# One attention block and one gated feed-forward block on one core: maxima tiles in pairs of banks until the first gate product, and query groups and the first projection as products over all rows

## The chip, the cores and the metric

The kernel runs on 1 core of one Trainium2 chip. Its engines are called as the profile calls them: PE (TensorE, the matrix products), PEld (TensorE's loads of weights), DVE (VectorE), ACT (ScalarE), POOL (GpSimd) and SP (SyncE, whose queue issues nearly all DMAs here). The time of a run is the device time in microseconds (us) of one execution. Half a per cent of this kernel's time is some 8 us.

## The reference

One layer on 2048 rows of width 512: an attention with 32 heads of 16 columns, which share one key and one value head, then a feed-forward block with 1792 gated columns. Each has a layer norm before it, which is scaled and shifted by vectors that are made from `c`, and a gate vector behind it.

```python
mod = (_silu(c) @ w_mod).reshape(c.shape[0], 6, 1, -1)
sa, ca, ga, sb, cb, gb = (mod[:, i] for i in range(6))      # written out in the source
h = _layernorm(x) * (1 + ca) + sa
q, k, v = (h @ wq, 32 heads of 16), h @ wk, h @ wv          # one k and one v for all heads
o = softmax(q k^T * 16 ** -0.5) v
x = x + ga * (o @ wo)
h = _layernorm(x) * (1 + cb) + sb
x = x + gb * ((sigmoid(h @ w_gate) * (h @ w_up)) @ w_down)
```

The inputs are fp32. The kernel splits operands into two fp16 parts, high and low, and adds three products (high with high, high with low, low with high) where the reference has one.

## The kernel before, in words

**Prologue** (some 105 us): loads, the vectors made from `c`, the first norm, keys, values and the first query groups. Its order stands in a table, PLAN.

**Main loop.** The queries are cut into 8 blocks of 256 rows, the heads into 4 groups of 8; such a pair is a *unit*, 32 in all. A unit has 16 *steps*, one for each 128 keys, so there are 512 steps, and a step has two *half-steps*. A half-step issues on PE, in this order (ORDER):

- `s0`, `s1`: two products of scores with the keys on the output's partitions (tile `st`, one bank of 512 columns each, two banks in turn). ACT takes the exponential of each into `P` (`st_tile`).
- `a0`, `a1`: two products of scores the other way round, for a later unit (tile `sa`, one bank each, three banks in turn). DVE takes the maximum of each over its 512 columns into one column of `mx` (`a_tile`, `a_max`). When a unit's 64 are done, the row maxima `m` go into the unit's query tile by way of HBM (`max_end` and what it defers), so that the exponential cannot overflow.
- `c`: the product of `P` with the values (`pv`), two steps behind, summed over the unit in the bank `craw`. It is fp32 and comes in two passes.
- a *piece* of other work (`piece`): some matmuls of the group that is on.

PE's array is used in two halves of 64 rows. Scores and maxima of a half-step run in one half, the value product in the other, each as four matmuls of 32 columns (`columns`). A group that needs 128 rows is a `Couple` of two groups in two banks: each half of the array does its part of one group and then of the other.

**The other work** has stages: `q`, the query groups that the prologue left (ten, as five couples); for each block of queries `wo`, the attention's projection (two groups of 128 rows of queries); `gu`, gate and up products; `dn`, the down products. `pick` takes the next one when its marks are old enough (the constants SKIP, GAP, EGAP, HGAP), `pace` sets how many matmuls a half-step gets, so that a block's work ends by step CHAIN of a later unit's row of four. Eight banks: `craw`, two `st`, three `sa`, two for groups.

**From a unit's end to the projection.** `unit_end` copies `craw` to `cs` (ACT). `place` then issues on SP two small DMAs of the denominators to HBM (`lD`) and eight copies of 16 rows each into `raw`. W1 steps later `recip` loads the denominators as `lc`, W2 steps later DVE takes their reciprocal `rc`, which goes back through HBM to `raw`, and W3 steps later `finish` (POOL) multiplies. SP issues in order, so a DMA that must wait holds back all behind it.

**From the projection to the gate products.** `wo_group`'s end scales by `ga`; `norm` and `norm2` (POOL, bn statistics on DVE) add the input and normalize, and make fp16 rows `h2r`; two transposing DMAs for each 128 rows turn them into `h2`, and the second of the two sets a mark. `ask` queues the loads of gate weights (`gw`), of which `drip` issues one a half-step.

Every matmul that goes through the recording class has line 143 in the profile, so tiles tell more than lines: `pq` is a query group, `po` the projection, `pgu` gate and up, `pd` down.

Of the kernel before, what the change touches and what calls it, by code (L numbers as in the profile page):

```python
# [9 lines left out]
F32 = mybir.dt.float32  # L10
AF = mybir.ActivationFunctionType
ALU = mybir.AluOpType
# [4 lines left out]
P = 128  # L17
# [12 lines left out]
NU = 4  # L30
# [29 lines left out]

SKIP = 9
GAP = 2
EGAP = 6
HGAP = 3
CHAIN = 26
QRATE = 1.1
MOST = 3
LEAST = 2.0  # L70
# [8 lines left out]
GLATE = 3  # L79
FIRST = 70  # L80
QLEAD = 6
W1 = 2
W2 = 3
W3 = 2

# [11 lines left out]
def adaln_mqa_glu_kernel(  # L97
# [106 lines left out]
    class Couple:  # L204
# [27 lines left out]
        def alone(self):  # L232
            for g in self.gs:
                g.alone()

    def t32(name, shape=(P, 512)):
        return wp.tile(list(shape), F32, tag="f32", name=name, bufs=18)
# [386 lines left out]
    def a_tile(i, n, held):  # L624
        a_max(*a_product(i, n, held))

    pend, seen = [], {}

    def max_end(i):
# [73 lines left out]
    def place(b, o, cs, lD, raw):  # L703
        for j in range(2):
            sp1.dma_start(lD[0].rearrange("(p r j) q -> j p r q", j=2, r=2)[j],
                          cs[DH + 64 * j:64 + 64 * j:32].rearrange("p (r q) -> p r q", r=2))
        for g in range(8):
            p_, r_, j = g // 4, g // 2 % 2, g % 2
            hh = 2 * j + p_
            sp1.dma_start(raw[DH * g:DH * (g + 1), :QU], cs[32 * hh:32 * hh + DH, r_ * QU:(r_ + 1) * QU])  # L710
        defer(W1, lambda: recip(b, o, lD, raw))

    def recip(b, o, lD, raw):
        lc = wp.tile([P, DH], F32, tag="lc", name="lc", bufs=2)
        rc = wp.tile([P, DH], F32, tag="rc", name="rc", bufs=2)
        sp1.dma_start(lc, lD[0].rearrange("h (s e) -> (h s) e", e=DH))

        def recip2():
            dve.reciprocal(rc, lc)
            sp1.dma_start(lD[1].rearrange("h (s e) -> (h s) e", e=DH), rc)  # L720
            defer(1, recip3)

        def recip3():
            sp1.dma_start(raw[:, QU:], lD[1].unsqueeze(1).to_broadcast([8, DH, QU]))
            defer(W3, lambda: finish(b, o, raw))

        defer(W2, recip2)
# [41 lines left out]
    def defer(n, f_):  # L769
        waits.append((now[0] + n, f_))  # L770
# [75 lines left out]
    def ffn_block(b, end_of_all=False):  # L846
# [4 lines left out]
        def wo_group(t):  # L851
            def term(n, rs):
                o, i = divmod(n, 3)
                a_, w_ = passes(*aTs[b, o], WO['woh'], WO['wol'])[i]
                return a_[rs, t * P:(t + 1) * P], w_[rs, o, :]

            def begin():
                xrs[t] = t32("xr")
                sp1.dma_start(xrs[t], x[b * QU + t * P:b * QU + (t + 1) * P, :])

            def end(po, second):
                xr, t1 = xrs.pop(t), t32("t1")
                if second:
                    act.activation(t1, po, AF.Identity)
                    pool.tensor_tensor(t1, t1, mods[2], op=ALU.mult)
                else:
                    dve.tensor_tensor(t1, po, mods[2], op=ALU.mult)
                if tail:
                    dve.tensor_tensor(xr, t1, xr, op=ALU.add)
                    row_norm([t1], [xr])  # L870
                    dve.tensor_tensor(t1, t1, mods[4], op=ALU.mult)
                    dve.tensor_tensor(t1, t1, mods[3], op=ALU.add)
                    x1[t] = xr, t1
                else:
                    defer(1 + t, lambda: norm(t, t1, xr))

            return Group("wo", 12, "po", term, end, begin)
# [5 lines left out]
        def norm2(t, t1, xr):  # L883
            row_norm([t1], [xr], later=True)
            x1[t] = xr, t1
            pool.tensor_tensor(t1, t1, mods[4], op=ALU.mult)
            pool.tensor_tensor(t1, t1, mods[3], op=ALU.add)
            rows = pair("h2r")
            pool.tensor_scalar(rows[:, 0], t1, 1.0, 0.0, op0=ALU.mult, op1=ALU.add)
            pool.tensor_tensor(rows[:, 1], t1, rows[:, 0], op=ALU.subtract)  # L890
            h2[t] = turned(rows, f"h2{t}")
            if b == 0 and t == 0:
                ask(0)
            defer(HLATE, h2[t][1])

        def turned(rows, name):
# [155 lines left out]
            gs[-1].after[12 + 6 * k + 5] = lambda spent=at + NDC * NPR + k + 1: ask(spent)  # L1052
        for g in gs:
            g.needs = [(b, "h20"), (b, "h21")]
        names = [f"g{p}{t}" for p in range(NPR) for t in range(2)] + [f"g{NPR}"]
        for ds in downs:
            gs.append(Couple(*ds))
        gs[-2].needs = [(b, z) for z in names[:2 * -(-HF // 4)]]
        gs[-1].needs = [(b, z) for z in names]
        first = Couple(*wos)  # L1060
        for g in [first, *gs]:
            g.b = b
        return first, gs


    alist = [(i, n) for i in range(len(units)) for n in range(64)]
# [38 lines left out]
    psum["ctx"].close()  # L1105
    psum["ctx"] = ExitStack()
    psum["s"] = psum["ctx"].enter_context(tc.tile_pool(name="pa", bufs=1, space=PSUM, reuse_waits="tile"))
    psum["b"], psum["n"], psum["banks"] = psum["s"], 7 - sum(SBANKS.values()), SBANKS
    P2 = ctx.enter_context(tc.tile_pool(name="w2", bufs=1, reuse_waits="tile"))
    WO["woh"] = P2.tile([P, 4, D], F16, name="woh")  # L1110
    WO["wol"] = P2.tile([P, 4, D], F16, name="wol")
# [8 lines left out]
    wjobs = weight_jobs()  # L1120
    nw, wdone = len(wjobs), 0
    qleft = [(b, o) for b in range(NB) for o in range(4) if (b, o) not in qdone]
    early = [Couple(q_group(*z), q_group(*y)) for z, y in zip(qleft[::2], qleft[1::2])]
    work, urgent = early, []
    run = []
    lead = [0.0]
# [21 lines left out]
    def pick(s):  # L1148
        if urgent and s >= urgent[0].ready:
            return urgent.pop(0)  # L1150
        if work and all(k in marks and s >= marks[k] + (EGAP if k == (0, "h21") else HGAP if k[1] == "h21" else GAP) for k in getattr(work[0], "needs", ())):
            return work.pop(0)

    def pace(s, g):
        if g.stage == "q":
            return QRATE, 2
        now_, late = s // (NU * NKB), s % (NU * NKB) >= CHAIN
        until = 2 * ((now_ + late) * NU * NKB + CHAIN)
        left = sum(z.n for z in [g, *urgent, *work] if late or z.b < now_ - 1 or z.stage == "wo") + 24 * late
# [43 lines left out]

    for i, (b, o) in enumerate(units):
        if o == 0 and b > 0:
            first_, rest = ffn_block(b - 1)
            first_.ready = i * NKB + SKIP
            urgent.append(first_)
            work.extend(rest)
        for kb in range(NKB):  # L1210
            s = i * NKB + kb
# [11 lines left out]
            for n in range(2):  # L1223
                t = kb - kb % 2 + n
                for z in ORDER:
                    k = int(z[1:] or 0)
                    if z[0] == "a" and an + 4 * n + 2 * k + 1 - h < len(alist):
                        a_tile(*alist[an + 4 * n + 2 * k + 1 - h], k == 1)
# [79 lines left out]
```

## Time and profile before

| | |
|---|---|
| median of three runs | 1629.62 us (1621.7, 1630.42, 1629.62) |
| the profiled execution, its own time | 1623.57 us |
| its span, first to last instruction | 1621.8 us, mean granted TensorE clock 0.991 |
| PE busy | 1576.0 us, 97% |
| DVE busy | 1415.9 us, 87%; 1295.7 of it the 2048 maxima, 684 ns each |
| ACT busy | 1265.9 us, 78%; 1159.8 of it the 2048 exponentials, 597 ns each |
| POOL busy | 666.1 us, 41% |
| DMA | 140.47 MB, mean 87 GB/s |

A busy share is one over the whole span. [...] A row "x8" groups instructions that follow each other; what stands behind "idle" or "<-" is what ended the engine's wait.

### The profile page before, as it was taken

How to read it: one execution, taken by the hardware profiler on the slowest of the kernel's cores; microseconds unless marked ns; L12 is line 12 of the kernel's file. 1: busy time of each engine (PE TensorE's matmuls, PEld its weight loads, DVE VectorE, ACT ScalarE, POOL GpSimd, SP SyncE). 2: the span in 40 equal slices, each digit the busy share in tenths (PEclk: the TensorE clock that was granted, in tenths of full speed). 3: DMA queues.
4: the chain of work that ended last, by engine and by line, in shares of the span. 5: the costliest groups of instructions: out<-in, count | busy, mean ns of one | idle time of the engine just before them, and what ended most of it. 6: DMA issues, size and time to landing. Idle time of an engine off the chain costs nothing.

```text
span 1621.8 us, 91775 instructions
## 1 busy us (share of the span) xinstructions
PE 1576.0 (97%) x41417; PEld 1000.9 (62%) x41417; DVE 1415.9 (87%) x2400; ACT 1265.9 (78%) x2293; POOL 666.1 (41%) x827
## 2 busy tenths in 40 slices
PE   6999999999999999999999999999999999999998
PEld 3335444556677666666666666676666666665465
DVE  7789999999999999999999999999999999993041
ACT  4538888888888888888888888888888888888600
POOL 5453787245326232443226232543226322533223
PEclk9989999999999999999999999999999999999999
DMA  7222554044521334125321334115411343124411
GB/s 235 76 84 65 164 157 132 28 119 113 133 68 36 81 85 109 29 41 130 95 62 33 90 85 107 34 36 128 111 44 43 80 113 95 21 50 120 116 66 53
DMA packets 185461, 140.47 MB, mean 87 GB/s; under 512 B 96628, under 2 KB 144748, under 8 KB 185068
## 3 DMA queue, kind: packets, MB, share of 16 engines
q1 hardware_dynamic: 185068, 134.60, 31.6%
q8 instruction: 324, 5.31, 1.4%
q14 instruction: 69, 0.57, 0.1%
HBM read 97.45 MB, written 16.50 MB: 70 GB/s over the span
## 4 chain that ended last, share of the span: by engine, by line
PE 83%; DVE 6%; ACT 5%; DMA 3%; SPq 2%; issue 2%; POOL 0%; POOLq 0%; ACTq 0%; DVEq 0%
PE craw L143 22%; PE pgu L143 16%; PE sa L143 14%; PE st L143 13%; PE pd L143 7%; DVE mx L143 4%; ACT P L143 3%; PE pq L143 2%; PE pgu L200 2%; PE pd L200 2%; PE po L143 2%; SPq L143 2%; ACT th L143 1%; DMA gw<-wD 1%; DMA lc<-lD 1%
## 5 line engine op out<-in xcount | busy, mean ns | idle before, releaser
L143 DVE TENSOR_REDUCE mx<-sa 128x1 f32<-128x512 f32 x2048 | 1295.7, 684 | 65.4 <-PE sa L143 51.2
L143 ACT ACTIVATE P<-st 128x512 f32<-128x512 f32 x2048 | 1159.8, 597 | 214.9 <-PE st L143 158.8
L143 PE MATMUL craw<-P,V 64*32 64x512 f32 x8192 | 1080.3, 593 | 0.4 <-ACT cs L143 0.3
L143 PE MATMUL st<-qp,kp 64*32 64x512 f16 x8192 | 833.4, 379 | 12.8 <-ACT P L143 7.8
L143 PE MATMUL sa<-kp,qp 64*32 64x512 f16 (+1 forms) x7940 | 648.2, 378 | 7.2 <-DVE mx L143 6.7
L143 PEld LDWEIGHTS <-kp 64*32 64x32 f16 x8192 | 335.4, 90 | 283.3 <-issue 113.4
L143 PE MATMUL pgu<-gw,h 64*32 64x512 f16 x9408 | 419.3, 376 | 3.9 <-DMA gw<-wD 1.3
L143 PEld LDWEIGHTS <-qp 64*32 64x32 f16 (+1 forms) x7940 | 252.9, 92 | 103.5 <-issue 45.0
L143 PEld LDWEIGHTS <-h 64*32 64x32 f16 (+1 forms) x9600 | 214.4, 92 | 81.9 <-issue 28.2
L143 PEld LDWEIGHTS craw<-P,V 64*32 64x32 f32 x8192 | 237.4, 105 | 20.2 <-issue 3.2
L143 PE MATMUL pd<-wdh,g 64*32 64x512 f16 x2688 | 136.0, 376 | 1.8 <-DVE t L143 1.6
L959 POOL TENSOR_SCALAR th<-th 128x512 f32<-128x512 f32 x49 | 30.3, 618 | 234.3 <-ACT th L143 214.4
L575 POOL MEMSET qp<- 32x1024 f16 x60 | 56.7, 944 | 118.7 <-PE st L143 116.4
L143 PEld LDWEIGHTS <-g 64*32 64x32 f16 x4032 | 83.2, 92 | 29.1 <-issue 7.1
L732 POOL TENSOR_TENSOR raw<-raw 128x256 f32<-128x256 f32 x31 | 22.8, 734 | 171.0 <-DMA raw<-lD 143.0
L143 PE MATMUL pd<-wdl,g 64*32 64x512 f16 x1344 | 79.4, 376 | 0.0
L143 DVE COPY u<-pgu 128x512 f32<-128x512 f32 (+1 forms) x49 | 31.6, 645 | 38.4 <-PE pgu L143 38.2
L960 POOL TENSOR_TENSOR th<-th,u 128x512 f32<-128x512 f32 x49 | 62.7, 1280 | 4.1
L1016 POOL TENSOR_TENSOR ot<-ot,gb 128x512 f32<-128x512 f32 x12 | 15.3, 1279 | 112.3 <-ACT ot L143 112.3
L963 POOL TENSOR_TENSOR gr<-th,gr 128x512 f16<-128x512 f32 x49 | 57.0, 1164 | 4.1
L143 PE MATMUL craw<-nought 64*32 64x1 f16 x357 | 58.2, 163 | 0.0
L143 PE MATMUL pq<-h,wdh 64*32 64x512 f16 (+1 forms) x688 | 54.9, 390 | 0.2
(154 smaller groups left out, 1097.5 us busy)
## 6 DMA issues: line engine op xcount, KB each, us to landing
gw<-wD SPq DMA_DIRECT2D x224, 256.0 KB
wD<-gw SPq DMA_DIRECT2D x28, 256.0 KB
wm<-in_w_mod_dram SPq DMA_DIRECT2D x6, 1024.0 KB
qp<-qD SPq DMA_DIRECT2D x192, 32.0 KB
qD<-q SPq DMA_DIRECT2D x16, 256.0 KB
xr<-in_A_x_dram SPq DMA_DIRECT2D x16, 256.0 KB
out_dram<-ot SPq DMA_DIRECT2D x16, 256.0 KB
raw<-cs SPq DMA_DIRECT2D x248, 16.0 KB
```

Of the source, the lines that this page charges most:

```text
L143: return (lambda *a, **k: keep(f_(*a, **k))) if pinned else f_
L200: pe.matmul(cut[0](self.bank) if cut else self.bank, l_, r_, start=(n == 0), stop=(n == self.n - 1))
L575: eng.memset(qp[j:j + 32], 0.0)
L732: keep(pool.tensor_tensor(raw[:, :QU], raw[:, :QU], raw[:, QU:], op=ALU.mult))
L959: pool.tensor_scalar(th, th, 1.0, 1.0, op0=ALU.add, op1=ALU.mult)
L960: pool.tensor_tensor(th, th, u_, op=ALU.mult)
L963: pool.tensor_tensor(rows[:, 1], th, rows[:, 0], op=ALU.subtract)
L1016: pool.tensor_tensor(ot, ot, mods[5], op=ALU.mult)
```

## The change

It has five parts.

1. **Pairs of banks.** Until the first gate group is taken, the banks are laid out as two `st`, one for groups and two tiles `sw` of two banks each. `a_half` puts `a0` and `a1` of a half-step into the two banks of one `sw`, and one DVE pass writes two columns of `mx`. At the first group that is not a `Whole`, `narrow` closes this layout and opens the old one.
2. **Products over all rows.** In that time groups have one bank. So the ten query groups and the first block's two projection groups are `Whole`: matmuls of 128 rows by 128 columns, instead of couples. A query group gets two matmuls in every second half-step, a projection group two in each of six half-steps.
3. **Earlier gate products for the first block.** The first of them needs the first 128 rows alone, a fixed gap of 3 steps stands behind marks of either rows (EGAP is no longer used), the projection may start a step earlier (SKIP, SKIP0), gate weights are asked for when the projection begins, and the first block's pace is set by CHAIN0.
4. **Denominators.** W1 goes from 2 to 1, and `recip`'s load of `lc` is issued before the last four of the eight copies.
5. **A pause.** When a projection is due within 4 steps, no other group is started.

```diff
-SKIP = 9
+SKIP, SKIP0 = 8, 8
-CHAIN = 26
+CHAIN, CHAIN0 = 26, 18
-W1 = 2
+W1 = 1
...
+    class Whole:
+        def __init__(self, g, b=0):
+            self.g, self.stage, self.n, self.w, self.after, self.b = g, g.stage, g.n, g.w, {}, b
+        def part(self, n0, n1):
+            self.g.alone(n0, n1)
...
+    def a_half(i, n, k, sw=[]):
...
+        if k == 0:
+            sw.append(psum["s"].tile([P, 2, 512], F32, tag="sw", name="sw", bufs=2))
+        l_, r_ = get_q(i)[64 * j:64 * j + 64, r, qt * P:(qt + 1) * P], kp[64 * j:64 * j + 64, kc * 512:(kc + 1) * 512]
+        columns(sw[0][:, k], l_, r_, True, True, 64 * j if k else None)
+        if k:
+            dve.tensor_reduce(mxs[i][:, 4 * j + r, qt, kc - 1:kc + 1], sw.pop(), axis=AX.X, op=ALU.max)
...
-        for g in range(8):
+        place_rows(cs, raw, range(4))
+        defer(W1, lambda: recip(b, o, cs, lD, raw))
...
         sp1.dma_start(lc, lD[0].rearrange("h (s e) -> (h s) e", e=DH))
+        place_rows(cs, raw, range(4, 8))
...
             def begin():
+                if b == 0 and t == 0:
+                    ask(0)
...
+        if b == 0:
+            gs[0].needs = gs[0].needs[:1]
...
-        first = Couple(*wos)
+        firsts = [Whole(z) for z in wos] if b == 0 else [Couple(*wos)]
...
-    psum["b"], psum["n"], psum["banks"] = psum["s"], 7 - sum(SBANKS.values()), SBANKS
+    psum["b"], psum["n"], psum["banks"] = psum["s"], 1, {"st": 2}
+    wide = [True]
+    def narrow():
+        wide.clear()
+        psum["ctx"].close()
+        psum["ctx"] = ExitStack()
+        psum["s"] = psum["ctx"].enter_context(tc.tile_pool(name="pm", bufs=1, space=PSUM, reuse_waits="tile"))
+        psum["b"], psum["n"], psum["banks"] = psum["s"], 7 - sum(SBANKS.values()), SBANKS
...
-    early = [Couple(q_group(*z), q_group(*y)) for z, y in zip(qleft[::2], qleft[1::2])]
+    early = [Whole(q_group(*z)) for z in qleft]
...
+        if urgent and s > urgent[0].ready - 4:
+            return None
-        if work and all(k in marks and s >= marks[k] + (EGAP if k == (0, "h21") else HGAP if k[1] == "h21" else GAP) for k in getattr(work[0], "needs", ())):
+        if work and all(k in marks and s >= marks[k] + (HGAP if k[1][:2] == "h2" else GAP) for k in getattr(work[0], "needs", ())):
...
-        now_, late = s // (NU * NKB), s % (NU * NKB) >= CHAIN
+        now_, late = s // (NU * NKB), s % (NU * NKB) >= (CHAIN if s >= 2 * NU * NKB else CHAIN0)
...
     def parts(s, hb, g):
+        if isinstance(g, Whole):
+            return [2, 0] * 6 if g.stage == "q" else [2] * 6 + [0]
...
+        if wide and not isinstance(g, Whole):
+            narrow()
```

Since the plan is made by rules, most of the move does not show in the diff. By the plan, counted in steps of the main loop, the query groups lie in steps 0 to 59 (before 1 to 62), the projection of the first block in 72 to 78 (before 73 to 79), the first gate product at 83 (before 92); from step 154 on both plans have the same work in the same steps, within one step.

DVE, second unit of the main loop, before: its queue from one unit's row maxima to the next (`mx` takes the maxima, `sa` is a bank of scores).

```order
L143 TENSOR_REDUCE mx<-sa 128x1 x40
L143 RECIPROCAL rc<-lc 128x16
L143 TENSOR_REDUCE mx<-sa 128x1 x22
L143 TENSOR_REDUCE m<-mx 128x16
L143 TENSOR_REDUCE mx<-sa 128x1 x2
```

And after, at the same place:

```order
L143 TENSOR_REDUCE mx<-sw 128x2 x18
L143 RECIPROCAL rc<-lc 128x16
L143 TENSOR_REDUCE mx<-sw 128x2 x13
L143 TENSOR_REDUCE m<-mx 128x16
L143 TENSOR_REDUCE mx<-sw 128x2
```

62 passes over one bank ahead of the row maxima became 31 over two, and the reciprocal stands one step's maxima earlier in the queue.

PE, the first piece of a query group in the main loop (`pq` a query group's bank, `wdh` its weights, `kp` the keys); a piece of the difference, `-` before and `+` after:

```order
 L143 LDWEIGHTS wdh
-L143 MATMUL pq<-h_383,wdh 32x512
+L143 MATMUL pq<-h_383,wdh 128x512
 L143 LDWEIGHTS wdh
-L143 MATMUL pq<-h_383,wdh 32x512
+L143 MATMUL pq<-h_383,wdh 128x512
+L143 LDWEIGHTS kp
+L143 MATMUL st<-qp,kp 32x512
```

Two matmuls that fill 128 output partitions stand between the scores, where a row of matmuls with 32 partitions each stood.

SP, where the tenth unit has ended, before (`gr` the gated rows that are transposed, `wD` gate weights in HBM, `qD` queries in HBM):

```order
L143 DMA lD<-cs 4x1x256 x2
L143 DMA raw<-cs 16x256 x8
L143 DMA_TRANSPOSE g_15301<-gr 128x4x128 x2
L143 DMA gw<-wD 128x1024 x2
L143 DMA lc<-lD 128x16
L143 DMA gw<-wD 128x1024 x2
L143 DMA qp<-qD 16x4x256 x6
```

And after, at the same place:

```order
L143 DMA lD<-cs 4x1x256 x2
L143 DMA raw<-cs 16x256 x4
L143 DMA_TRANSPOSE g_13949<-gr 128x4x128 x2
L143 DMA lc<-lD 128x16
L143 DMA raw<-cs 16x256 x4
L143 DMA gw<-wD 128x1024 x4
L143 DMA qp<-qD 16x4x256 x6
```

The load of `lc` moved ahead of four copies and of two loads of gate weights; the four copies and all gate weights now stand behind it.

More of the change, by code (lines that the diff above doesn't have):

```diff
@@ L625, in a_tile @@
         a_max(*a_product(i, n, held))
+    def a_half(i, n, k, sw=[]):
+        if i not in mxs:
+            mxs[i] = wp.tile([P, 8, 2, 4], F32, tag="mx", name="mx", bufs=2)
+        kc, qt, j, r = spot(i, n)
+        if k == 0:
[3 more added lines that the diff above has]
+        if k:
+            assert kc % 2 == 1
+            dve.tensor_reduce(mxs[i][:, 4 * j + r, qt, kc - 1:kc + 1], sw.pop(), axis=AX.X, op=ALU.max)
+            seen[i] = seen.get(i, 0) + 2
+            if seen[i] == 64:
+                pend.append((i,))
     pend, seen = [], {}
@@ L706, in place, with place_rows @@
                           cs[DH + 64 * j:64 + 64 * j:32].rearrange("p (r q) -> p r q", r=2))
-        for g in range(8):
+        place_rows(cs, raw, range(4))
+        defer(W1, lambda: recip(b, o, cs, lD, raw))
+    def place_rows(cs, raw, gs):
+        for g in gs:
             p_, r_, j = g // 4, g // 2 % 2, g % 2
@@ L710, in place, with recip @@
             sp1.dma_start(raw[DH * g:DH * (g + 1), :QU], cs[32 * hh:32 * hh + DH, r_ * QU:(r_ + 1) * QU])
-        defer(W1, lambda: recip(b, o, lD, raw))
-    def recip(b, o, lD, raw):
+    def recip(b, o, cs, lD, raw):
         lc = wp.tile([P, DH], F32, tag="lc", name="lc", bufs=2)
@@ L891, in norm2 @@
             h2[t] = turned(rows, f"h2{t}")
-            if b == 0 and t == 0:
-                ask(0)
             defer(HLATE, h2[t][1])
@@ L1059, in ffn_block @@
         gs[-1].needs = [(b, z) for z in names]
-        first = Couple(*wos)
-        for g in [first, *gs]:
+        firsts = [Whole(z) for z in wos] if b == 0 else [Couple(*wos)]
+        for g in [*firsts, *gs]:
             g.b = b
-        return first, gs
+        return firsts, gs
     alist = [(i, n) for i in range(len(units)) for n in range(64)]
@@ L1205, in adaln_mqa_glu_kernel @@
         if o == 0 and b > 0:
-            first_, rest = ffn_block(b - 1)
-            first_.ready = i * NKB + SKIP
-            urgent.append(first_)
+            firsts, rest = ffn_block(b - 1)
+            for z in firsts:
+                z.ready = i * NKB + (SKIP if b > 1 else SKIP0)
+            urgent.extend(firsts)
             work.extend(rest)
@@ L1227, in adaln_mqa_glu_kernel @@
                     if z[0] == "a" and an + 4 * n + 2 * k + 1 - h < len(alist):
-                        a_tile(*alist[an + 4 * n + 2 * k + 1 - h], k == 1)
+                        at = alist[an + 4 * n + 2 * k + 1 - h]
+                        if wide:
+                            a_half(*at, k)
+                        else:
+                            a_tile(*at, k == 1)
                     if z == "c" and vq:
```

## The prediction

> **What bounds the kernel now.** I read the rows of busy time by stage first, because the change ends at the first gate product. The columns are the stretch in us from the start, its length, then the busy us of TensorE, its weight loads, VectorE, ScalarE and GpSimd.
>
> ```profile
> 106.20:265.60 159.40, 153.87 (x3829) 79.34 (x3818) 150.51 (x255) 137.21 (x255) 103.05 (x130) 0.97 0.44 127
> 265.60:296.10 30.50, 27.83 (x630) 13.02 (x619) 29.05 (x52) 27.25 (x52) 20.24 (x26) 1.00 0.20 58
> 296.10:325.20 29.10, 27.93 (x736) 16.26 (x727) 28.77 (x51) 25.67 (x48) 8.89 (x13) 1.00 0.08 27
> 325.20:348.10 22.90, 21.98 (x459) 9.37 (x450) 22.86 (x41) 19.83 (x38) 14.58 (x18) 1.00 0.55 148
> 348.10:522.50 174.40, 173.45 (x5237) 120.92 (x5233) 166.89 (x278) 148.72 (x268) 73.49 (x88) 1.00 0.36 87
> ```
>
> These are the stage of the query groups (A, 60 steps; four exponentials a step), 12 steps after it (B), 11 steps with the first projection (C), 9 without other products, and 62 from the first gate product until both plans meet (E). VectorE is busy 94 to 100% up to the gate products; behind them TensorE is busy 99%. So I read next how dense each really is, in the timeline of one stretch of A.
>
> ```profile
> 183.41 0.40 PE L143 MATMUL st<-qp,kp 64*32 64x512 f16 x4 [0.29 <-ACT P L143]
> 183.86 0.60 ACT L143 ACTIVATE P<-st 128x512 f32<-128x512 f32 x1
> 184.21 4.23 DVE L143 TENSOR_REDUCE mx<-sa 128x1 f32<-128x512 f32 x7
> 184.51 0.40 PE L143 MATMUL st<-qp,kp 64*32 64x512 f16 x4
> 184.54 0.63 PE L143 MATMUL craw<-P,V 64*32 64x512 f32 x4
> 184.72 0.61 PE L143 MATMUL sa<-kp,qp 64*32 64x512 f16 x8
> 184.99 0.61 PE L143 MATMUL craw<-P,V 64*32 64x512 f32 x4
> 185.31 0.40 PE L143 MATMUL st<-qp,kp 64*32 64x512 f16 x4
> 185.42 0.51 PE L143 MATMUL pq<-h,wdh 64*32 64x512 f16 x8
> 186.95 0.40 PE L143 MATMUL st<-qp,kp 64*32 64x512 f16 x4
> ```
>
> Seven reductions follow each other in 4.23 us. With 0.68 us for the last, one starts every (4.23 - 0.68) / 6 = 0.592 us. Four a step are 2.37 us, and this step takes 186.95 - 184.51 = 2.44: VectorE sets its pace. TensorE needs less. Its two halves of rows work side by side: one does two score products and two maxima products, four times some 0.215 us, the other the value product in two passes 0.45 us apart (184.54 and 184.99), so 0.89 us in a half-step, which lasts 1.2. The query piece (185.42) lies in the rest.
>
> **The change part by part.** *Pairs of banks.* 166 passes over 1024 columns take the place of 332 over 512. No row shows one of 1024. The nearest are two sizes of a copy from PSUM.
>
> ```profile
> L143 DVE COPY u<-pgu 128x512 f32<-128x512 f32 x42 | 28.7, 682 | 25.1 <-PE pgu L143 25.1
> L143 DVE COPY u<-pgu 128x256 f32<-128x256 f32 x7 | 2.9, 418 | 13.2 <-PE pgu L143 13.2
> ```
>
> 256 columns more cost 682 - 418 = 264 ns in a row's duration, though 512 further ones cannot cost more than a whole second pass, 0.592 us. From below 2 x 0.264 = 0.528, so a pair takes 1.12 to 1.184 us in sequence. I take 1.13: 0.055 saved a pair, 0.11 a step. From both sides that is 0 to 0.13 a step. [...]
>
> *Query groups and first projection over all rows.* In 60 half-steps of A and 12 of C two products of 128 rows take the place of pieces on both halves. The prologue has such products between ones of 64 rows.
>
> ```profile
> 88.16 0.39 PE L143 MATMUL sa<-kp,qp 64*128 64x512 f16 x1
> 88.48 0.61 PE L143 MATMUL pq<-h,wdh 128*128 128x512 f16 x2
> 88.71 0.10 PEld L143 LDWEIGHTS <-wdl 128*128 128x128 f16 x1
> 88.92 0.38 PE L143 MATMUL pq<-h,wdl 128*128 128x512 f16 x1
> 89.23 0.39 PE L143 MATMUL sa<-kp,qp 64*128 64x512 f16 x2
> ```
>
> From 64 rows to 128 it is 0.32 us from start to start (88.16 to 88.48), back 0.31 (88.92 to 89.23), against 0.215 within one kind: 0.10 lost at each turn. And both halves must have ended. A half-step with such a piece takes 0.89 + 0.10 + 2 x 0.215 + 0.10 = 1.52 us, where VectorE now needs 1.13. The other half-step cannot make it up wholly: a bank of st goes round in 184.51 - 183.41 = 1.10 us (product, 0.45 until its exponential at 183.86, 0.60 for that, 0.05), and each half-step uses both banks once. So it takes 1.10, and a step of A takes 2.62 us, set by TensorE and st's banks, not by VectorE. A: 60 x 2.62 = 157.2. Beside 60 steps of 2.44 (146.4) the stretch now holds 13 us of beginnings and unit ends; VectorE's part of them is then hidden, and I keep 6. After, 163.2 against 159.4: 3.8 us slower. Bounds: VectorE alone sets the pace, 60 x (2 x 1.13 + 0.07 for its small passes) + 6 = 146, 13 faster; or the piece costs more (below). B has no such pieces: 24 x 1.13 + 1.5 for small passes and the unit's copy on ScalarE is 28.6 against 30.5, 1.9 faster. C: 12 x 1.52 + 10 x 1.13 = 29.5, and 1.0 for emptying the pairs where the banks are laid out anew (0 to 3; between, about one reduction with its waits), so 30.5 against 29.1: 1.4 slower. C's second projection is now evicted by VectorE (one pass of 0.68 more) and not by ScalarE and GpSimd; TensorE's pieces cover it.
>
> *Gate products from step 83, not 92.* The work is the same, spread over 71 steps where TensorE sets the time.
>
> ```profile
> L143 PE MATMUL craw<-P,V 64*32 64x512 f32 x996 | 131.1, 592 | 0.0
> L143 PE MATMUL pgu<-gw,h 64*32 64x512 f16 x1344 | 57.4, 376 | 0.1
> L143 PE MATMUL pd<-wdh,g 64*32 64x512 f16 x448 | 22.2, 376 | 0.3 <-DVE t L143 0.3
> L143 PE MATMUL pd<-wdl,g 64*32 64x512 f16 x224 | 13.1, 376 | 0.0
> L143 PE MATMUL po<-woh,a 64*32 64x512 f16 x128 | 6.7, 377 | 0.0
> L143 PE MATMUL po<-wol,a 64*32 64x512 f16 x64 | 3.8, 377 | 0.0
> L143 DVE TENSOR_REDUCE mx<-sa 128x1 f32<-128x512 f32 x248 | 158.3, 684 | 7.1 <-PE sa L143 5.6
> ```
>
> 1344 + 448 + 224 + 128 + 64 = 2208 products of 64 rows by 32 columns, eight at a time, are 276 x 0.215 = 59.3 us. The rest of the 174.4, 115.1 in 62 steps, is 1.856 a step. From step 83 on: 71 x 1.856 + 59.3 = 191.1 us, against 22.9 + 174.4 = 197.3: 6.2 faster. VectorE allows it: 284 x 0.592 + 8.6 (166.89 less 158.3) = 177. Work can be late there: the first rows' norm.
>
> ```profile
> 315.81 0.68 DVE L143 TENSOR_TENSOR t<-po,ga 128x512 f32<-128x512 f32 x1
> 331.32 1.16 POOL L890 TENSOR_TENSOR h2r<-t,h2r 128x512 f16<-128x512 f32 x1
> 336.35 6.24 SPq L143 DMA_TRANSPOSE h<-h2r  x4
> ```
>
> From the projection's copy to the rows it takes 332.48 - 315.81 = 16.7 us, 6.9 steps; two of four transposes 3.1 more on SP, now ahead of the next unit's copies instead of behind them and its q loads. The plan leaves 8 steps from the copy (75) to the product (83), 19.5 us against 19.8 and a landing. So TensorE waits, in order, 0 to 3 us; I take 1.0, since gate weights asked for at step 72 leave it no other reason: 5.2 faster.
>
> *The denominators one step earlier, four of eight copies behind them.* In before the load lc waits on SP behind eight copies and whatever is queued in that step, and VectorE waits for it, with every reduction behind.
>
> ```profile
> DVE rc L143 <- DMA lc<-lD: 12.9, 8, 5.5
> 544.24 1.09 SPq L143 DMA_DIRECT2D lD<-cs  x2
> 545.38 6.08 SPq L143 DMA_DIRECT2D raw<-cs  x8
> 551.57 3.67 SPq L143 DMA_TRANSPOSE g<-gr  x2
> 555.34 2.09 SPq L143 DMA_DIRECT2D gw<-wD  x2
> 557.48 0.42 SPq L143 DMA_DIRECT2D lc<-lD  x1
> 560.16 0.25 DVE L143 RECIPROCAL rc<-lc 128x16 f32<-128x16 f32 x1 [1.52 <-DMA lc<-lD]
> 740.67 0.25 DVE L143 RECIPROCAL rc<-lc 128x16 f32<-128x16 f32 x1 [1.90 <-DMA lc<-lD]
> ```
>
> Now lc stands behind four copies and, in such a unit, the two transposes: 3.0 + 2.1 = 5.1 us earlier (half of 6.08, and the gate weights' 2.09), while the reciprocal comes one step (2.8) earlier. That is 2.3 us more room than waits of 1.5 and 1.9 need. Of 12.9 us the one of 5.5 lies in the last unit, where no maxima follow; 7.4 remain in seven places. Bounds 0 (TensorE's own work covers them) and 7.4; I take 5.0, since TensorE at 99% has nothing that does not pass the maxima's banks. What is late next is the second four copies and the gate weights, which keep their place behind the same sum of issues.
>
> **Sum.** -3.8 + 1.9 - 1.4 + 5.2 + 5.0 = 6.9 us faster. The profiled execution took 1623.57; the change 1616.7. The three timed ones (1621.7, 1630.42, 1629.62) and it have a mean of 1626.3, 2.7 above it, so I forecast 1619.4, written 1619, against the median of 1629.62.
>
> **The rivals.** *VectorE keeps the pace in A and C.* For it: its 94 to 100% above, and value products that start ahead of the maxima products that precede them (184.54 against 184.72), so TensorE may hide turns. Against: the round of st's banks. A takes 146 and C 11 x 2.33 + 1 = 26.6: 17 and 4 less, 1598.
>
> *The two gains behind C do not come.* The gate products find h2 or weights late, and the stalls at rc pass to the gate weights behind them on SP. For it: SP's queue without a gap from 544 to 558. Against: 2.3 us of room. Then 1619.4 + 10.2 = 1629.6, no change. That the change doesn't do what it says is excluded for the pairs by the order below the diff; that one pass over two banks costs no less than two is the bound of 1.184, which moves B and C by 2 us alone.
>
> *Slower: the weights of a whole product are not loaded ahead.* Each of the 144 products in pieces, 72 pairs, then waits for its own 128 columns, 0.10 us (88.71): 0.20 a piece, 72 x 0.20 = 14.4, and as much again where the next small loads wait in turn, 0.10: 1619 + 14 to 1619 + 22, so 1637. It decides from 0.14 a piece on (10.2 / 72). Against it: 88.48 to 88.92 holds two products in 0.44 us with such loads hidden. [...]
>
> **How the numbers follow.** Forecast 0.46 (1612 to 1626), VectorE's pace 0.22, no gain 0.19, slower 0.13. The range 1600 to 1632 takes in the forecast, no gain and the nearer part of the two others. Half a per cent, 8 us, is about what a measurement of this kernel tells from no change: below 1621.5 and above 1637.8. Faster: 0.36 of the forecast, 0.22 and 0.02 of no gain, 0.60. Slower: 0.07 of the slower rival and 0.03 of no gain, for lateness beyond what I priced, 0.10. Same: the rest, 0.30.
>
> **What would show it.** A pair's pass of 1.2 us that starts every 1.25 to 1.35, with VectorE idle before it for TensorE, shows A right; passes 1.13 apart without idle time show the first rival. Steps of A that take 2.62 on average, C of 30.5, the stretch from step 83 to 154 of 191, and no wait of rc for lc above 0.3 us would show the terms. Whole products over 0.25 us apart within a piece show the slower rival. The forecast is wrong if A moves by more than 8 us either way, or if a wait of gate products for h or gw of over 2 us appears at the start.

## The result, and the profile after

The changed kernel takes 1638.85 us, median of 9 runs (1633.05 to 1643.28); the kernel before, measured beside it, 1627.07 (1621.70 to 1630.42, 9 runs). The ratio is 1.0072, 95% interval 1.0051 to 1.0093: **slower by 0.7%**, some 12 us, where 1619 and faster was forecast. The profiled execution took 1639.63 us, its span is 1637.7, at a granted clock of 0.99 as before.

The first view is again busy time by stage, of the changed kernel, cut at the same steps as the rows of before: A (query groups), B (nothing beside), C (first projection), steps 83 to 91, and 92 to 153. The columns are stretch, length, then the busy us of PE, PEld, DVE, ACT, POOL.

```profile
106.20:283.10 176.90, 170.84 (x3016) 63.78 (x3010) 144.87 (x133) 143.70 (x256) 106.78 (x135) 0.97 0.40 116
283.10:314.00 30.90, 28.43 (x595) 12.78 (x584) 29.44 (x29) 26.79 (x51) 16.65 (x21) 1.00 0.17 49
314.00:346.00 32.00, 31.23 (x571) 11.44 (x559) 29.11 (x32) 25.68 (x47) 15.33 (x22) 1.00 0.46 147
346.00:371.00 25.00, 24.55 (x725) 16.36 (x712) 23.89 (x38) 21.08 (x39) 12.35 (x15) 1.00 0.26 43
371.00:542.90 171.90, 170.16 (x4974) 113.09 (x4958) 164.62 (x278) 146.69 (x268) 68.03 (x81) 1.00 0.35 79
```

Beside the rows of before (159.40, 30.50, 29.10, 22.90, 174.40; cut exactly at step 60, as the rows of after and of the experiments are, its A is 158.8 and its B 31.0):

| stage | before | forecast | after | after less before |
|---|---|---|---|---|
| A | 159.4 | 163.2 | 176.9 | +17.5 |
| B | 30.5 | 28.6 | 30.9 | +0.4 |
| C | 29.1 | 30.5 | 32.0 | +2.9 |
| steps 83 to 153 | 197.3 | 192.1 | 196.9 | -0.4 |
| all behind, up to the span's end | 1099.3 | 1094.3 | 1094.8 | -4.5 |

The sum is +15.9, the difference of the two spans (1637.7 - 1621.8). So the loss is in A, and the one clear gain is behind step 154. These are traces of one execution each. From step 83 to 153 the traces of the six kernels with the changed plan (the changed kernel, e1, e2, e5, e7 and e10) lie between 194.7 and 198.8 us, so the 0.4 there is no gain that could be told from none.

In the groups of the changed kernel, a pass over a pair of banks and what VectorE waited for ahead of it:

```profile
L143 DVE TENSOR_REDUCE mx<-sw 128x2 f32<-128x1024 f32 x167 | 199.2, 1219 | 36.2 <-PE st L143 29.0 <-PE sw L143 4.1 <-PE craw L143 1.5
L143 DVE RECIPROCAL rc<-lc 128x16 f32<-128x16 f32 x31 | 7.5, 242 | 6.4 <-DMA lc<-lD 6.4
```

VectorE stands idle 36.2 us ahead of 167 passes: it waits mostly for products. The wait at the reciprocal has fallen from 12.9 us in 8 places to 6.4 in one.

The timeline of one stretch of A, after; first PE's products:

```profile
225.68 0.40 PE L143 MATMUL st<-qp,kp 64*32 64x512 f16 x4
226.01 0.39 PE L143 MATMUL pq<-h,wdl 128*128 128x512 f16 x1
226.23 0.38 PE L143 MATMUL pq<-h,wdh 128*128 128x512 f16 x1
226.54 0.40 PE L143 MATMUL st<-qp,kp 64*32 64x512 f16 x4
226.57 0.63 PE L143 MATMUL craw<-P,V 64*32 64x512 f32 x4
226.77 0.60 PE L143 MATMUL sw<-kp,qp 64*32 64x512 f16 x8
227.02 0.61 PE L143 MATMUL craw<-P,V 64*32 64x512 f32 x4
227.20 0.39 PE L143 MATMUL st<-qp,kp 64*32 64x512 f16 x4
...
227.70 0.40 PE L143 MATMUL st<-qp,kp 64*32 64x512 f16 x4
227.73 0.63 PE L143 MATMUL craw<-P,V 64*32 64x512 f32 x4
227.91 0.61 PE L143 MATMUL sw<-kp,qp 64*32 64x512 f16 x8
228.18 0.61 PE L143 MATMUL craw<-P,V 64*32 64x512 f32 x4
228.53 0.40 PE L143 MATMUL st<-qp,kp 64*32 64x512 f16 x4
228.86 0.39 PE L143 MATMUL pq<-h,wdh 128*128 128x512 f16 x1
```

The exponentials of the same stretch on ACT, with the idle time ahead of them:

```profile
227.05 0.60 ACT L143 ACTIVATE P<-st 128x512 f32<-128x512 f32 x1 [0.27 <-PE st L143]
227.88 1.69 ACT L143 ACTIVATE P<-st 128x512 f32<-128x512 f32 x3 [0.24 <-PE st L143]
```

And the passes over pairs of banks on DVE:

```profile
224.97 2.36 DVE L143 TENSOR_REDUCE mx<-sw 128x2 f32<-128x1024 f32 x2 [0.47 <-PE st L143]
227.77 2.36 DVE L143 TENSOR_REDUCE mx<-sw 128x2 f32<-128x1024 f32 x2 [0.44 <-PE st L143]
```

Two passes in 2.36 us are 2.36 - 1.22 = 1.14 from start to start: a dense pass over two banks costs what the prediction took (1.13), but ahead of each two VectorE waits 0.44 to 0.47. The piece's turns cost what it took too: st to piece 0.33, within the piece 0.22, piece to st 0.31. What it did not have is the second score product of a half-step. It starts at 227.20 and its exponential at 227.88, 0.68 later (its lag), while the one at 226.54 is followed after 0.51. Two st banks take turns, so this bank's next product (228.53) waits for that exponential's end (227.88 + 0.60 = 228.48). From the starts of the score products of steps 4 to 57, a half-step with a piece lasts 1.69 us on average and one without 1.19; forecast were 1.52 and 1.10.

The chain of waits tells what set the pace: it goes back from the last instruction, at each one to what released it, and gives the shares of the stretch by line. Of A before:

```profile
by line: PE craw L143 27.4%; PE st L143 23.8%; PE pq L143 16.1%; PE sa L143 15.9%; ACT P L143 7.4%; DVE mx L143 4.8%; issue 2.1%; ACT q L143 2.1%; ACT cs L143 0.4%; DVE m L143 0.3%; ACTq L143 0.1%; ACT mm L143 0.0%
```

And after:

```profile
by line: PE st L143 24.5%; ACT P L143 23.0%; PE craw L143 16.5%; PE pq L143 15.3%; PE sw L143 9.9%; DVE mx L143 3.4%; ACT q L143 3.3%; issue 3.0%; ACT cs L143 0.7%; ACTq L143 0.2%; DVE m L143 0.2%; ACT mm L143 0.0%
```

The reductions are a small part in both, already before the change; the exponentials' share grew from 7.4 to 23.0%.

### The profile page after: what moved, and what is told of

Its sections match the earlier page's. It is cut to its first block, busy times and chain, and to the rows that moved or that the text cites. A ratio compares the mean times of both kernels' runs of the same rounds, so it can differ in the third digit from the quotient of the medians.

```text
span 1637.7 us, 89559 instructions
## 1 busy us (share of the span) xinstructions
PE 1592.8 (97%) x40400; PEld 980.8 (60%) x40400; DVE 1408.3 (86%) x2234; ACT 1271.2 (78%) x2292; POOL 665.1 (41%) x826
## 4 chain that ended last, share of the span: by engine, by line
PE 82%; ACT 7%; DVE 5%; DMA 3%; issue 2%; SPq 1%; POOL 0%; POOLq 0%; ACTq 0%
PE craw L143 22%; PE pgu L143 16%; PE st L143 14%; PE sa L143 12%; PE pd L143 7%; ACT P L143 5%; DVE mx L143 3%; PE pq L143 2%; PE pgu L200 2%; PE pd L200 2%; PE po L143 2%; DMA gw<-wD 2%; PE sw L143 1%; ACT th L143 1%; DMA xall<-in_A_x_dram 1%
## 5 line engine op out<-in xcount | busy, mean ns | idle before, releaser
L143 DVE TENSOR_REDUCE mx<-sa 128x1 f32<-128x512 f32 x1714 | 1093.7, 683 | 61.2 <-PE sa L143 41.0
L143 PE MATMUL sa<-kp,qp 64*32 64x512 f16 (+1 forms) x6604 | 540.1, 377 | 4.7 <-DVE mx L143 4.6
L143 PEld LDWEIGHTS <-kp 64*32 64x32 f16 x8192 | 327.2, 90 | 318.4 <-issue 149.0
L143 PEld LDWEIGHTS <-qp 64*32 64x32 f16 (+1 forms) x7940 | 246.8, 93 | 85.1 <-issue 30.1
L143 DVE TENSOR_REDUCE mx<-sw 128x2 f32<-128x1024 f32 x167 | 199.2, 1219 | 36.2 <-PE st L143 29.0
L143 PE MATMUL sw<-kp,qp 64*32 64x512 f16 x1336 | 104.9, 384 | 0.0
```

The source lines that it names most:

```text
L143: return (lambda *a, **k: keep(f_(*a, **k))) if pinned else f_
```

## The experiments

**Pairs or pieces: e1.** Single banks, three for maxima and two for groups, as before; the query groups and the projection stay products over all rows.

```diff
-    psum["b"], psum["n"], psum["banks"] = psum["s"], 1, {"st": 2}
-    wide = [True]
+    psum["b"], psum["n"], psum["banks"] = psum["s"], 7 - sum(SBANKS.values()), SBANKS
+    wide = []
```

> The changed kernel, but the maxima keep single banks (three sa, two group banks) from the start; query groups and first projection stay products over all rows. Stage A (steps 0 to 60) took 159 us before and 177 after. Theory T (pieces over all rows: their turns, their waiting for both halves and the round of the st banks set A's pace): A stays at 177 within 3 us, half-steps with a piece at 1.69 us, plain ones at 1.19. Rival R (the pairs of banks lengthen A: a pass begins only after its second product and holds two banks): A falls to 160 to 163.

Measured: 1636.31 us (one run). A and B by stage:

```profile
106.28:281.41 175.13, 170.32 (x3016) 65.61 (x3010) 152.53 (x253) 143.71 (x256) 106.96 (x136) 0.97 0.41 117
281.41:311.68 30.27, 28.19 (x599) 12.44 (x584) 29.89 (x53) 26.76 (x51) 16.47 (x20) 1.00 0.19 50
```

A stays at 175.1, with half-steps of 1.69 and 1.17. The pairs are not what slows A, and they bring nothing either: A and B together are 205.4 here and 207.8 with pairs.

**One product a half-step: e2.** The pieces of a query group are spread, one product in each half-step instead of two in every second.

```diff
-            return [2, 0] * 6 if g.stage == "q" else [2] * 6 + [0]
+            return [1] * 12 + [0] if g.stage == "q" else [2] * 6 + [0]
```

> The changed kernel with one product over all rows in each of 12 half-steps, then one half-step without, in place of two in every second half-step: twice as many turns. Theory T: a half-step has a floor of 1.19 us from the st banks anyway, so a short piece in each hides its turn there: s0 to s1 0.66, then 0.66 to the next s0 (0.87 less one product of 0.215), 1.33 us a half-step, 2.66 a step, A about 167 instead of 177, total 10 us less than the changed kernel. Rival (the turns alone are the price, 0.20 us each pair): 60 more of them, A about 189, total 12 us more.

Measured: 1634.66 us, median of 10 (ratio to before 1.0036, 1.0017 to 1.0055; before 1626.86, 25 runs, shared with e4 and e8).

```profile
107.62:278.72 171.10, 165.43 (x3006) 69.20 (x3001) 149.93 (x133) 141.71 (x255) 105.44 (x134) 0.97 0.40 117
```

A falls by 5.8 us although the number of turns is doubled: half-steps of 1.38 and 1.39, 2.78 a step instead of 2.88; theory T had said about 167 for A, the rival 189. A group now takes 13 half-steps, so 9 of the 120 products lie behind step 60, and B is 1.1 longer (32.0): A and B together fall by 4.7. So turns alone don't explain what is missing; uneven half-steps are part of it. By the two ratios, 1.0036 and 1.0072, half of the loss against before is left.

**The denominators alone: e4.** The kernel before with the earlier load of denominators and four of the eight copies behind it, nothing else.

```diff
-W1 = 2
+W1 = 1
...
-        for g in range(8):
+        place_rows(cs, raw, range(4))
+        defer(W1, lambda: recip(b, o, cs, lD, raw))
...
-        defer(W1, lambda: recip(b, o, lD, raw))
...
         sp1.dma_start(lc, lD[0].rearrange("h (s e) -> (h s) e", e=DH))
+        place_rows(cs, raw, range(4, 8))
```

> The kernel before with the denominators' part alone (W1 of 1, the load of lc ahead of the last four copies). If the part is worth what the changed kernel shows from step 154 on (4.0 us gained there), it is 3 to 5 us faster than before, and VectorE waits under 1 us for lc apart from the last unit. Rival: the stalls only show where TensorE has slack, or pass on to the gate weights; then no difference within 1.5 us.

Measured: 1621.01 us, median of 10 (1614.61 to 1623.45), ratio 0.9969 (0.9949 to 0.9989). The wait that the edit is for, in its trace:

```profile
DVE rc L143 <- DMA lc<-lD: 2.1, 1, 2.1
```

5.9 us faster by the medians, where 5.0 was forecast for this term. Here one wait is left of eight, at the last reciprocal (1496.91 us). It has the lowest median of all kernels that leave nothing out.

**Denominators and early gate products: e8.** The kernel before with the denominators and the gate products from step 83, in single banks and with couples.

```diff
-SKIP = 9
+SKIP, SKIP0 = 8, 8
...
-CHAIN = 26
+CHAIN, CHAIN0 = 26, 18
...
-W1 = 2
+W1 = 1
...
+                if b == 0 and t == 0:
+                    ask(0)
...
+        if b == 0:
+            gs[0].needs = gs[0].needs[:1]
...
+        if urgent and s > urgent[0].ready - 4:
+            return None
...
```

> The kernel before with the denominators' part and the early gate products of the first block (marks, SKIP, CHAIN0, gate weights asked for with the projection, the pause), but couples and single banks throughout. My forecast for the early gate products was 5 us; the changed kernel shows 0.5 us from step 83 to 154, 1.3 of it lost at step 83. If that loss belongs to the new layout of the banks, this gains 1 to 3 us over the denominators' part alone; if spreading gains nothing because steps do not get shorter below some 2.65 us, it equals it within 1 us.

Measured: 1624.61 us, median of 10, ratio 0.9990 (0.9967 to 1.0013): no more gain than e4, by the medians 3.6 us worse, where 1 to 3 better or the same was expected. From step 83 to 154 it takes 204.2 us (7.9 us of this in step 111, 6.2 in step 124), before 197.3. The waits between 370 and 420 us:

```profile
POOL wst L345 <- DMA wst<-in_B_w_down_dram: 25.7, 3, 11.3
ACT P L143 <- PE st L143: 11.8, 22, 5.3
DVE mx L143 <- PE sa L143: 7.1, 4, 5.5
PEld L143 <- DMA qp<-mD: 5.8, 1, 5.8
PE st L143 <- DMA qp<-mD: 5.1, 1, 5.1
```

Score products wait 5.1 us for a unit's row maxima, which come through SP's queue. No row of the changed kernel shows such a wait between 340 and 560 us, so it belongs to this mixture. In step 124 TensorE stands 3.1 us ahead of a maxima product and waits for nothing that the profile shows. With these two stalls the run can't tell what the gate products alone are worth.

**Short value products: e7.** The changed kernel; it leaves out work: the value products of a unit's middle blocks cover 64 of 512 columns in the first 60 steps.

```diff
-            z = pe.matmul(c_[32 * hh:32 * hh + 32, :], V[rs, t, :], Ps[i, t, hh][rs, :], start=start, stop=stop)
+            w_ = 64 if 0 < t < NKB - 1 and now[0] < 60 else 512
+            z = pe.matmul(c_[32 * hh:32 * hh + 32, :w_], V[rs, t, :], Ps[i, t, hh][rs, :w_], start=start, stop=stop)
...
+            dve.tensor_scalar(lc, lc, 1e-20, None, op0=ALU.max)
```

> This kernel leaves out work: in the first 60 steps of the main loop the value products of the middle blocks cover 64 of their 512 columns (and the denominators get a floor, one small pass on VectorE a unit, so that no reciprocal is infinite); pieces, pairs and all else are as in the changed kernel. Question: why a half-step with a query piece takes 1.69 us and not 1.52. Theory S (a score product's end reaches ScalarE only when the value product issued ahead of it on the other half of the rows has ended, so the second exponential starts 0.68 us behind its product and not 0.44): the lag falls to about 0.45, the half-step with a piece to 1.45 to 1.56, the other half-step to 1.10 to 1.15, and the stage of the query groups from 176.9 to 160 to 167 us. Rival T (the turns between 64 and 128 rows and the products between them cost what is missing): the lag may fall, but the half-step with a piece stays above 1.62 and the stage above 172.

Its one run took 1634.01 us, which is no measure, as work is left out. A:

```profile
106.47:275.20 168.73, 160.93 (x3017) 64.25 (x3013) 146.38 (x136) 143.43 (x257) 106.51 (x135) 0.97 0.42 122
```

A falls by 8.2 us, to 168.7, just above the range of theory S and well below the rival's. The second exponential of a half-step without a piece starts 0.50 behind its product (median) instead of 0.68; the half-step with a piece lasts 1.57 on average and 1.51 in the median, the forecast 1.52; that without one 1.18, hardly changed and not the 1.10 to 1.15 that S gave. In a half-step with a piece the two score products start 0.82 apart in the changed kernel and 0.65 here (medians), and from the second one to the half-step's end it is 0.86 in both. So the price of a piece was rightly worked out; what was missing lies ahead of the second score product, whose bank waits for the late exponential. The lag is 0.68 behind a value product of 512 columns and 0.50 behind one of 64; by what way the value product delays the exponential, the traces do not show.

**Without query pieces: e5 and e6.** Both leave out work: of each query group's products in the main loop only the first and the last are issued, 2 of 12, in the changed kernel (e5) and in the same way in the kernel before (e6).

```diff
+                if self.stage == "q" and 0 < n < self.n - 1:
+                    continue
```

> This kernel leaves out work: of the 12 products of each query group in the main loop only the first and the last are issued, two of twelve; all else is as in the changed kernel, pairs included. With it goes the same cut in the kernel before (the next run). If the query pieces over all rows are what costs, the stage of the query groups takes at most 60 x (2 x 1.13 + 0.07) + 9 = 149 us and a little for the pieces left (up to 155), against 176.9 with them: a piece then costs 0.3 to 0.4 us of the step. If the pairs of banks themselves slow the stage, it stays above 165.

In the kernel before it reads:

```diff
+                    if self.stage == "q" and 0 < n % m < m - 1:
+                        continue
```

> This kernel leaves out work: of the 24 products of each couple of query groups in the main loop only the first two and the last two are issued; all else is as in the kernel before. If products on both halves of the rows ride under VectorE's pace there, the stage of the query groups stays within 3 us of 159.4 (156 to 160). If they cost time of their own, it falls by 6 us or more. The stage here less the stage of the run before this one is what pairs of banks are worth where no pieces lie: forecast 0.11 a step, 6 to 7 us; 0 if a pass over two banks saves nothing in sequence.

One run each took 1620.64 us (e5) and 1625.63 (e6), the kernel before beside them 1623.17.

A of e5, pairs and nearly no pieces:

```profile
104.97:266.17 161.20, 149.63 (x2917) 66.10 (x2910) 145.43 (x133) 138.09 (x257) 105.07 (x133) 0.97 0.44 127
```

A of e6, single banks and nearly no pieces:

```profile
106.86:262.90 156.04, 145.13 (x3053) 66.17 (x3046) 149.64 (x253) 136.56 (x255) 103.72 (x131) 0.98 0.44 128
```

The pieces left out cost 15.7 us in the changed kernel (176.9 - 161.2) and 2.8 in the one before (158.8 - 156.0): there they ride along on both halves. And without pieces the pairs are 5.2 us slower than single banks, not 6 to 7 faster. Neither theory had that; e5's 161.2 lies between the two expectations. Part of it are the 20 products over all rows that e5 keeps, but B, which has none, shows no gain either.

What sets the pace without pieces is told by the chain of waits of stage B alone. Of the kernel before:

```profile
by line: ACT P L143 35.0%; PE st L143 20.2%; PE craw L143 19.2%; PE sa L143 8.2%; issue 6.1%; DVE mx L143 3.9%; ACT q L143 3.5%; PE pq L143 2.4%; ACT cs L143 2.0%; DVE m L143 0.5%; ACTq L143 0.3%; ACT mm L143 0.1%
```

Of the changed kernel:

```profile
by line: ACT P L143 37.0%; PE st L143 22.0%; PE craw L143 18.4%; PE sw L143 8.6%; issue 7.7%; DVE mx L143 4.0%; ACT cs L143 2.0%; DVE m L143 0.4%; ACTq L143 0.4%; ACT mm L143 0.1%
```

The reductions are 4% of it in both, and the median step (61 to 70) takes 2.44 us before and 2.45 after: the passes became cheaper and the step did not. The chain runs through score product, exponential, and the bank that becomes free. VectorE was nearly as dense beside it, which its busy share of 95% showed; but it was not what ended the waits.

**A third bank for scores: e10.** The changed kernel with single banks, shared out until the first gate product as three st, three for maxima and one for pieces.

```diff
-    psum["b"], psum["n"], psum["banks"] = psum["s"], 1, {"st": 2}
+    psum["b"], psum["n"], psum["banks"] = psum["s"], 1, {"st": 3, "sa": 3}
...
-                        if wide:
+                        if False:
```

> The changed kernel with single banks of maxima as in e1, and the banks until the first gate product shared out as three for score products (st, two before), three for maxima and one for the pieces; nothing is left out. Theory R (two st banks go round in 1.2 us or more, since a score product's end is signalled late, and this wait, not VectorE and not the turns, sets a half-step without a piece and holds the one with it): the waits of score products for an exponential go, a half-step with a piece falls from 1.69 to about 1.5, the stage of the query groups from e1's 175.2 to 155 to 165 us, and the 12 steps behind it from 30.3 to at most 30. The time then falls below the changed kernel's by 10 to 18 us, to about that of the kernel before. Rival T (the products over all rows and their turns are what TensorE lacks): the stage stays above 171, and the time within 6 us of the changed kernel's.

Measured: 1624.84 us, median of 10 (1622.48 to 1627.95) against 1625.67 (13 runs) before, ratio 0.9992 (0.9979 to 1.0006). A and B by stage:

```profile
106.17:271.44 165.27, 163.86 (x3021) 60.18 (x3017) 151.86 (x253) 138.49 (x256) 106.36 (x134) 0.97 0.43 124
271.44:300.90 29.46, 29.04 (x587) 12.12 (x575) 29.31 (x53) 26.22 (x51) 17.36 (x22) 1.00 0.18 51
```

The chain of waits of its A:

```profile
by line: PE craw L143 33.6%; PE st L143 28.9%; PE pq L143 20.5%; PE sa L143 14.2%; DVE mx L143 1.1%; ACT cs L143 1.1%; issue 0.6%
```

With one bank more for the scores (and one less for pieces) A is 9.9 us shorter than e1's and B 0.8; the time is back at that of the kernel before, 14 us below the changed kernel's. It is no better than that although it has the denominators' gain: A is still 6.5 us longer than before (165.3 against 158.8). The exponentials are gone from the chain. So the round of the two st banks is shown to be what cost A these 10 us. Theory R expected 155 to 165 and got 165.3, just beyond its upper end, and its expectation on the pieces was wrong: a half-step without a piece takes 0.91 now, but one with a piece 1.77, not 1.5. The chain is now TensorE's alone, 2.68 a step against 0.89 + 1.52 = 2.41 from the prediction's two prices. The timeline of PE shows where a piece costs more:

```profile
228.37 0.40 PE L143 MATMUL st<-qp,kp 64*32 64x512 f16 x4
228.70 0.39 PE L143 MATMUL pq<-h,wdh 128*128 128x512 f16 x1
...
230.88 0.60 PE L143 MATMUL craw<-P,V 64*32 64x512 f32 x3
230.89 0.37 PE L143 MATMUL st<-qp,kp 64*32 64x512 f16 x1
230.90 0.59 PE L143 MATMUL craw<-P,V 64*32 64x512 f32 x1
230.90 0.38 PE L143 MATMUL st<-qp,kp 64*32 64x512 f16 x3
231.42 0.61 PE L143 MATMUL pq<-h,wdh 128*128 128x512 f16 x2
```

From the last start ahead of a piece to the piece it is 0.33 where a score product ran alone (228.37 to 228.70), but 0.52 where a pass of the value product started with it (230.90 to 231.42). Of the 54 pieces of steps 4 to 57, 27 lie so, 0.52 in the median, and 24 behind a score product alone, 0.31. The changed kernel agrees: none of its pieces starts less than 0.52 behind the last matmul of a value product's pass (0.60 long), while a maxima product on the other half starts 0.20 behind such a pass (226.57 to 226.77).

## Why the prediction was wrong

**What bounds A and B** is the step that failed first. The prediction read VectorE's pace from a busy share of 94 to 100% and from seven dense reductions. Both readings are right and do not answer the question. The chain of waits of the stage itself, which was not read, gives the reductions 5% in A and 4% in B, and TensorE 83% in A. The exponential's way round the two st banks, TensorE and VectorE were so near each other that a cheaper VectorE was worth nothing: B takes 30.9 with pairs, against 31.0 cut at the same steps, and not 28.6.

**A's two half-steps** is the term of the sum that was mis-sized: 60 x (1.52 + 1.10) was 60 x (1.69 + 1.19), 0.26 a step or 15.6 us; the beginnings, taken as 6, came to 4.1, which makes the 13.7 by which A missed. The bank's round of 1.10 came from one row of before, in which the exponential started 0.45 behind its product. The same stretch of before has another one, behind the product of 184.06:

```profile
184.66 2.24 ACT L143 ACTIVATE P<-st 128x512 f32<-128x512 f32 x4 [0.21 <-PE st L143]
```

That is 0.60, with ScalarE idle ahead of it. Over steps 4 to 57 of before 0.44 is the shortest lag, and the median of those for which ScalarE stood idle is 0.59. After, the medians are 0.51 behind a half-step's first product and 0.68 behind its second, where there is no piece. With value products of 64 columns (e7) the second lag is 0.50, and a third bank (e10) takes 10 us of the stage away. The first lag is 0.51 in e7 too; why it is not 0.45 stays open, and with it most of the 0.09 by which the half-step without a piece was short. The 13 us of before beside 60 steps of 2.44 were misread as well: 2.44 is the median of steps 4 to 57, their mean is 2.60, so that only some 3 us are left for beginnings. The mechanism named, TensorE and st's banks and not VectorE, was right; its size and the value product's part in it were not.

**C** took 32.0 where its half-steps alone were put at 29.5. The twelve with a piece last 1.59 instead of 1.52 (0.8), the ten without 1.30 instead of 1.13 (1.7). The 1.0 for the banks' new layout fell into step 83.

**Gate products earlier** was forecast at 5.2 and brought 0.4. The term took 1.856 us a step plus 0.215 for eight small products and had no floor of its own. But steps without any such products take 22.90 / 9 = 2.54 us in before, with VectorE at 22.86 of 22.90. Over 71 steps instead of 62 more of them lie near that floor, and what a lighter step saves on TensorE VectorE keeps; it is busy 188.5 of the 196.9 us. This cause is argued from the rows and no run takes it apart. Two more steps stand out in the changed kernel, 97 (4.15 us) and 145 (3.70), where no step of the stretch takes over 3.5 before; what they lack was not followed, so the plan's unevenness is a rival. One part is seen: step 83 lasts 3.86 us, against 2.60 in e1, where the banks aren't laid out anew at this point. So that costs 1.3, near the 1.0 that the prediction put into C. No product of step 83 waits for gate weights or the norm: the lateness at the start, which the prediction feared, didn't come.

**The denominators** were right in mechanism and size: 5.0 forecast, 4.5 behind step 154 after the change and 5.9 alone in e4. Behind step 154 the eight traces with this part take 1090.2 to 1096.6 us, the two without it 1099.2 and 1101.4. The 2.3 us of room were the whole gain, not what was left beyond waits of 1.5 and 1.9 (0.4); the waits went all the same. That the last unit's wait would stay was right too (6.4 of the 12.9).

**The rivals.** VectorE's pace (1598) fell. "No gain" was right for the gate products, wrong for the denominators. The slower rival had the right sign and very nearly the time, 1637, by a mechanism that did not happen: products within a piece are 0.22 apart (226.01 to 226.23), below the 0.25 that would have shown it. The weights are loaded beside running products: the second product's load starts at 226.02 and takes 0.10, where the first product starts at 226.01 and the second at 226.23. A pair of banks is 1.14 from start to start against 2 x 0.592, 0.04 saved where 0.055 was taken. The rival that was needed stood in the text as a term of the sum: st's banks, with a higher price.

## What to carry to other kernels

Ask the chain of waits of a stage, not only its busy shares, what a faster engine is worth there: in B of before TensorE was busy 91, VectorE 95 and ScalarE 89% of the time, and each could be taken for the bound. Products over all rows cost more than their own time here, where two halves of the array work side by side: two of 0.22 made a half-step 0.50 longer (1.69 against 1.19), and 0.86 in e10 (1.77 against 0.91), where a piece starts 0.52 behind a pass of the value product and 0.31 behind a score product alone. With two banks in turn a long and a short half-step took 2.88 a step and two even ones 2.78 (e2). Price a bank's round by the usual lag in the trace (0.59 here), not by one row (0.45), and before spending banks on wider passes, try one more bank for the round itself (e10 did so with products over all rows; with couples it was not tried).

## What was not expected of the hardware

- The exponential behind a half-step's second score product starts 0.68 us after it in the changed kernel, where a value product of 512 columns on the other half of the rows was issued ahead, and 0.50 where that is 64 columns wide (e7). Why is not shown.
- A change from 64 to 128 rows takes 0.33 us from start to start ahead of the first product and 0.31 behind the last, where products within a piece start 0.22 apart (the changed kernel, 225.68 to 226.54), but 0.52 ahead of it if a pass of an fp32 product has just begun on the other half (e10, 230.90 to 231.42).
- A VectorE pass over 1024 columns in two PSUM banks took 1.22 us, and 1.14 from start to start in sequence (the changed kernel, the two of 224.97); two over 512 took 2 x 0.592 = 1.18 from start to start (before, the seven of 184.21).
